# Attention and MLP-mixer on one core: the loads of the fourth batch's k and q moved ahead of a tail transpose on the DMA queue

The kernel runs on one core of one Trainium2 chip (trn2). The metric is device time in microseconds (us) of one execution, lower is better. A DMA queue is here the list of copies and transposes that the Sync engine (SP) issues, in program order.

## The reference

Eight batches go through a linear attention with cosine weights and then a token and channel mixer. Cut to what matters:

```python
def _attn_ref(q, k, v):                     # 8 batches x 8 heads x 576 rows x 64, float32
    theta = np.pi / 2.0 * pos / S
    def phi(x, c, s):
        r = np.maximum(x, 0.0)
        return np.concatenate([r * c, r * s], axis=-1)
    q_p, k_p = phi(q, cos_w, sin_w), phi(k, cos_w, sin_w)
    kv = np.einsum('bhsf,bhsd->bhfd', k_p, v)
    z = np.sum(k_p, axis=2)
    num = np.einsum('bhsf,bhfd->bhsd', q_p, kv)
    den = np.einsum('bhsf,bhf->bhs', q_p, z)[..., None] + 1e-06
    return num / den

def _moe_ref(x, w_tok1, w_tok2, w_ch1, w_ch2):          # 256 token, 1536 channel units
    h = np.maximum(x.transpose(0, 2, 1) @ w_tok1, 0.0) @ w_tok2
    u = x + h.transpose(0, 2, 1)
    return u + np.maximum(u @ w_ch1, 0.0) @ w_ch2
```

## The kernel before

The channel mixer of one batch fills TensorE for a period of some 27 us. The work for the next two batches is hooked into that period's slots (a slot follows each group of matmuls). In the first period the channel mixer of batch 0 runs, in the second that of batch 1; the first nm of batch 2 comes in slot 6 of the second. Batches are counted from 0 in the code and from one in the text, so "the fourth batch" is `3`. JA is 5, the blocks of 128 rows that a batch's 576 rows fill.

Names in the lines of the profile: PE is TensorE, ACT ScalarE, DVE VectorE, POOL GpSimd, SPq the Sync engine's DMA queue. qp and kp are the weighted features of q and k, qpT is qp transposed, kv is the product of kp and v, and nm that of qpT and kv. u is what the channel mixer takes in and uT its transpose; c_ps are the mixer's first matmuls, o_ps its second.

```python
    def load(b, t):                           # k, q or v of a batch: two copies, 640 + 512 KB
        x = raw_of(t, b)                      # k and q: two buffers by b % 2; v: one
        ...
            dmas.append(nc.sync.dma_start(out=x[par::2, :, :n * D], in_=...))

        def q_turn(self, j, n):               # batches 2 to 7: transposed by the DMA queue
            if self.b in Q_DMA:
                nc.sync.dma_start_transpose(out=self.qpT[:, j * H:(j + n) * H, :], in_=...)
                return
        ...
        def num(self, j):                     # nm: needs qpT and kv
            for h in range(H):
                nc.tensor.matmul(nm[...], self.qpT[:, j * H + h, :], self.kv[:, h, :D + 1], ...)
        ...
        def mix2(self, g, turn=True):         # last part, g = 2: the batch's last 64 rows
                ...
                if self.c == 1:
                    utb = one.tile([P, Dm], BF16, name="utb")
                    nc.gpsimd.tensor_copy(utb, u_tail[:, i, :])
                    nc.sync.dma_start_transpose(out=uT_tail[:, i], in_=utb)   # tail transpose

    def first_hooks(n, n2):                   # n: batch 1, n2: batch 2
        ...
        at(12, load, 2, "v")
        ...
        for g in range(3):
            at(19 + g, n.mix2, g)             # g = 2 in slot 21: the tail transpose
        at(19, n2.q_feature, 0)
        at(20, n2.q_feature, 1)
        at(21, load, 3, "k")
        at(21, load, 3, "q")
        ...
    # at the end of the period: the stores of batch 0, four copies of 256 KB

    def second_hooks(n, m):                   # n: batch 2, m: batch 3
        ...
        at(0, n.q_turn, 0, 2)                 # three transposes of batch 2's q
        at(1, n.q_turn, 2, 2)
        at(2, n.q_turn, 4, 1)
        at(5, n.kv_mm)
        at(5, load, 3, "v")
        at(5, load, 4, "k")
        at(5, load, 4, "q")
        for j in range(JA):
            at(6 + j, n.num, j)
        ...
        at(13, load, 4, "v")                  # ahead of batch 2's u transposes (mix2)
```

## Time and profile before

| | before |
|---|---|
| median of three runs | 287.91 us (286.62 to 288.2) |
| the profiled run | 286.91 us, span 285.1 us, mean granted TensorE clock 0.981 |
| TensorE busy | 265.3 us, 93% of the span |
| wait of the third batch's first nm | 7.91 us |

How to read it: TensorE is the bound over the whole span, so the question is only where it stands still and why. The wait is in TensorE's own timeline (start, length, line, operation, names, shapes, count; in brackets the idle time before it and what ended it):

```profile
69.72 1.02 PE L392 MATMUL c_ps<-uT,wc_135 128*128 128x512 bf16 x4
78.65 0.62 PE L280 MATMUL nm<-kv,qpT 128*128 128x65 bf16 x8 [7.91 <-DMA qpT<-qp]
```

The prediction below shows the page's rows, the chain of waits and the DMA queue around this wait.

### The profile page before, as it was taken

What the parts mean: (1) busy time and instruction counts of PE and PEld (TensorE: products, weight loads), DVE (VectorE), ACT (ScalarE), POOL (GpSimd) and SP (SyncE); (2) the same over time, 40 slices, a digit from 0 to 9 for tenths busy, and PEclk for the clock granted to TensorE, in tenths of its full rate; (3) what the DMA queues carried; (4) which work ended last, traced back from release to release, by engine and by line L of the source; (5) the groups of instructions that cost most, each with busy time, mean ns of one, the idle gap of its engine ahead of it and who ended that gap; (6) DMA issues with size and microseconds to landing.
All of it is one profiled execution on the core that took longest, in us unless ns stands there. A gap on an engine that the chain in (4) does not pass through costs nothing.

```text
span 285.1 us, 4653 instructions
## 1 busy us (share of the span) xinstructions
PE 265.3 (93%) x1834; PEld 133.0 (47%) x1834; DVE 168.0 (59%) x333; ACT 119.6 (42%) x176; POOL 55.3 (19%) x81
## 2 busy tenths in 40 slices
PE   8879989989099999999999999999999999999994
PEld 3454455444044454446444644464455444444443
DVE  4774884496055966794578459955866562322422
ACT  2973594339114733914490548055705201301300
POOL 4472420070003510250042004400200030000000
PEclk9999999999669999999999999999999999999999
DMA  6999998709999999999969994960493063003012
GB/s 212 318 165 288 356 210 260 255 20 286 284 232 359 238 227 277 344 207 212 347 185 217 254 365 94 196 165 2 90 218 101 0 94 126 21 0 149 0 51 97
DMA packets 78726, 53.62 MB, mean 188 GB/s; under 512 B 47792, under 2 KB 76016, under 8 KB 78704
## 3 DMA queue, kind: packets, MB, share of 16 engines
q1 hardware_dynamic: 74688, 49.06, 62.8%
q0 software_dynamic: 3616, 3.74, 8.2%
q10 hardware_dynamic: 400, 0.52, 0.5%
q8 instruction: 14, 0.23, 0.3%
q14 instruction: 8, 0.07, 0.1%
HBM read 35.78 MB, written 9.44 MB: 159 GB/s over the span
## 4 chain that ended last, share of the span: by engine, by line
PE 82%; DMA 7%; ACT 5%; DVE 3%; issue 1%; POOL 0%; ACTq 0%; POOLq 0%; DVEq 0%
PE c_ps L392 30%; PE o_ps L424 28%; PE u_ps L343 5%; PE nm L280 4%; DMA qpT<-qp 3%; DMA vt_77<-in_v_dram 3%; PE o_ps L404 3%; PE kv_ps L265 3%; ACT qp L236 2%; ACT qpT L256 1%; DVE x L288 1%; PE ut_ps L355 1%; PE o_ps L416 1%; PE b_1001 L300 1%; PE b_692 L300 1%; PE b_2301 L300 1%
## 5 line engine op out<-in xcount | busy, mean ns | idle before, releaser
L392 PE MATMUL c_ps<-uT,wc_135 128*128 128x512 bf16 x384 | 95.1, 384 | 1.1 <-ACT uT L376 1.1
L392 PEld LDWEIGHTS <-wc_135 128*128 128x128 bf16 x432 | 40.0, 98 | 44.4 <-issue 3.1
L348 POOL CAST ub<-u 128x1024 bf16<-128x1024 f32 x14 | 14.7, 1049 | 131.2 <-DVE u L345 91.7
L427 DVE TENSOR_TENSOR u<-o_ps,u 128x512 f32<-128x512 f32 x28 | 19.2, 687 | 21.5 <-PE o_ps L424 21.5
L288 DVE TENSOR_TENSOR x<-nm,den 128x512 bf16<-128x512 f32 x40 | 27.7, 691 | 1.4
L280 PE MATMUL nm<-kv,qpT 128*128 128x65 bf16 x320 | 17.2, 197 | 9.9 <-DMA qpT<-qp 7.9
L284 DVE TENSOR_SCALAR den<-nm 128x8 f32<-128x8 f32 x40 | 6.6, 165 | 31.7 <-PE nm L280 31.7
L280 PEld LDWEIGHTS <-qpT 128*128 128x128 bf16 x320 | 15.1, 100 | 21.0 <-DMA qpT<-qp 9.1
L345 DVE TENSOR_TENSOR u<-u_ps,x 128x1024 f32<-128x1024 f32 x16 | 19.5, 1221 | 5.1 <-PE u_ps L343 5.0
L223 POOL CAST vbf_125<-vt_77 128x512 bf16<-128x512 f32 x18 | 12.3, 725 | 24.0 <-DMA vt_77<-in_v_dram 22.3
L236 ACT ACTIVATE qp<-qt_79,bias_108,cos_t 128x512 bf16<-128x512 f32 x20 | 15.9, 804 | 0.0
L236 ACT ACTIVATE qp<-qt_76,bias_108,cos_t 128x512 bf16<-128x512 f32 x19 | 15.0, 802 | 0.3 <-DMA qt_76<-in_q_dram 0.3
L265 PEld LDWEIGHTS <-kp 128*128 128x128 bf16 x320 | 11.3, 97 | 3.5 <-issue 1.2
L404 PE MATMUL o_ps<-wc_139,h_441 128*128 128x512 bf16 x48 | 12.3, 379 | 0.0
L396 ACT ACTIVATE h_2730<-c_ps 128x512 bf16<-128x512 f32 x6 | 3.6, 597 | 20.6 <-PE c_ps L392 20.6
L236 ACT ACTIVATE qp<-qt_76,bias_108,sin_t 128x512 bf16<-128x512 f32 x15 | 12.0, 802 | 0.0
L236 ACT ACTIVATE qp<-qt_79,bias_108,sin_t 128x512 bf16<-128x512 f32 x15 | 12.0, 802 | 0.0
L215 DVE TENSOR_SCALAR kp<-kt_75,cos_t 128x512 bf16<-128x512 f32 x18 | 10.3, 570 | 2.7 <-DMA kt_75<-in_k_dram 2.7
L396 ACT ACTIVATE h_844<-c_ps 128x512 bf16<-128x512 f32 x9 | 5.1, 593 | 16.0 <-PE c_ps L392 16.0
L215 DVE TENSOR_SCALAR kp<-kt_78,sin_t 128x512 bf16<-128x512 f32 x20 | 11.6, 580 | 0.0
L138 PE MATMUL wm<-zero 128*128 128x512 bf16 x38 | 10.1, 429 | 1.3 <-POOL zero L70 1.3
L215 DVE TENSOR_SCALAR kp<-kt_78,cos_t 128x512 bf16<-128x512 f32 x20 | 11.3, 567 | 0.0
(151 smaller groups left out, 397.0 us busy)
## 6 DMA issues: line engine op xcount, KB each, us to landing
out_dram<-u SPq DMA_DIRECT2D x32, 256.0 KB, 2.6
vt_77<-in_v_dram SPq DMA_DIRECT2D x8, 640.0 KB, 9.4
vt_77<-in_v_dram SPq DMA_DIRECT2D x8, 512.0 KB, 8.6
kt_75<-in_k_dram SPq DMA_DIRECT2D x4, 640.0 KB, 5.6
qt_76<-in_q_dram SPq DMA_DIRECT2D x4, 640.0 KB, 8.1
kt_78<-in_k_dram SPq DMA_DIRECT2D x4, 640.0 KB, 6.4
qt_79<-in_q_dram SPq DMA_DIRECT2D x4, 640.0 KB, 8.5
kt_75<-in_k_dram SPq DMA_DIRECT2D x4, 512.0 KB, 4.6
```

Of the source, the lines that this page charges most:

```text
L215: eng.tensor_scalar(dst, src, scalar1=tab, scalar2=0.0, op0=ALU.mult, op1=ALU.max)
L236: nc.scalar.activation(self.qp[:, j, :, f, :], src, AF.Relu, bias=bias0, scale=tab[:, self.c, j:j + 1])
L265: nc.tensor.matmul(kv_ps[:, g, hh * (D + 1):(hh + 1) * (D + 1)], self.kp[:, j, h].rearrange("p f d -> p (f d)"), self.vb[:, j, h, :D + 1], ...
L280: nc.tensor.matmul(nm[:, h // HH, c0:c0 + D + 1], lw, self.kv[:, h, :D + 1], start=True, stop=True)
L288: nc.vector.tensor_mul(self.x[:, j, :].rearrange("p (g h d) -> p g h d", g=2, h=HH), nmv[:, :, :, :D], den_b)
L343: nc.tensor.matmul(u_ps[:, jj], w2[:, self.c, ki, 2 * g + jj, :], self.B1[:, ki, :], start=(ki == 0), stop=(ki == NT - 1))
L345: nc.vector.tensor_add(self.u[:, js, :], u_ps, self.x[:, js, :])
L348: nc.gpsimd.tensor_copy(self.ub[:, js, :], self.u[:, js, :])
L392: nc.tensor.matmul(c_ps, wc1[:, ki, mi * P:(mi + 1) * P], uT[:, :, ki, :], start=(ki == 0), stop=(ki == NCC - 1))
L404: nc.tensor.matmul(o_ps[j], h1[:, ki, j * P:(j + 1) * P], wc2[:, ki, :], start=(ki == 0), stop=(ki == NCH - 1))
L424: nc.tensor.matmul(o_ps, h1[:, ki, j * P:(j + 1) * P], wc2[:, ki, :], start=(ki == 0), stop=(ki == NCH - 1))
L427: nc.vector.tensor_add(u[:, j, :], o_ps, u[:, j, :])
```

## The change

The intent: k and q of the fourth batch fill buffers that have long been free, yet on the queue they stand behind the tail transpose, which waits for its input. Then they stand in front of the third batch's q transposes, which TensorE needs at once. Issued eight slots sooner, they go ahead of the tail transpose. The whole diff:

```diff
         at(19, n2.q_feature, 0)
         at(20, n2.q_feature, 1)
-        at(21, load, 3, "k")
-        at(21, load, 3, "q")
+        at(13, load, 3, "k")
+        at(13, load, 3, "q")
         if 1 in U_PE:
```

## The prediction

> **What bounds the kernel now.** I read the page first, for the engine that is busy and for slices in which it is not. The first row is TensorE's busy share in 40 slices of 7.1 us, the second its granted clock, the third the DMA engines:
> ```profile
> PE   8879989989099999999999999999999999999994
> ...
> PEclk9999999999669999999999999999999999999999
> DMA  6999998709999999999969994960493063003012
> ```
> TensorE is busy 265.3 of 285.1 us, so it is the bound. Three things stand out: TensorE's eleventh slice (71 to 78 us) is a 0, the only one; its clock fell in the eleventh and twelfth; and the DMA engines have a slice of 0 just before, the ninth (57 to 64 us). Nothing else in the row of the clock is low.
>
> Next I read the chain of work that ended last, in order of time, around those slices (start us, length us, what):
> ```profile
> 68.22 0.48 ACT h_844 L396
> 68.70 0.25 ACT qp L236
> 68.95 9.65 DMA qpT<-qp
> 78.60 0.05 issue
> 78.65 0.62 PE nm L280 x8
> 79.27 1.71 PE c_ps L392 x4
> 80.98 0.44 PE nm L280 x8
> 81.42 1.71 PE c_ps L392 x4
> 83.12 0.46 PE b_1001 L300 x2
> ```
> From 88 us to the end at 281 the chain is all TensorE with pieces of "issue" under 0.3 us. Before 88 us its largest piece by far is this transpose of the third batch's q on the DMA queue. It ends a TensorE wait of 7.91 us (the timeline's figure, 70.74 to 78.65), and the two groups of four c_ps matmuls after it take 1.71 us each where the same group takes 0.86 in the rest of the chain: half clock.
>
> Why is the transpose late? The DMA queue's own timeline (start, length of the issue, not of the transfer):
> ```profile
> 45.86 1.32 SPq L87 DMA_DIRECT2D vt_77<-in_v_dram  x2
> 61.87 1.27 SPq L365 DMA_TRANSPOSE uT_tail<-utb  x1
> 63.19 1.28 SPq L87 DMA_DIRECT2D kt_78<-in_k_dram  x2
> 64.52 1.48 SPq L87 DMA_DIRECT2D qt_79<-in_q_dram  x2
> 66.09 2.76 SPq L439 DMA_DIRECT2D out_dram<-u  x4
> 68.95 11.51 SPq L242 DMA_TRANSPOSE qpT<-qp  x3
> 80.56 1.43 SPq L87 DMA_DIRECT2D vt_77<-in_v_dram  x2
> ```
> The queue sat 14.7 us behind the tail transpose, which waits for its input (the queue's waits call it 15.7 us, L365 on POOL). When that came, k and q of the fourth batch, the stores of the first batch and the three q transposes all went out in one burst. Of the 11.51 us of the three transposes, the first alone took 7.56. The amounts of data tell the rest:
> ```profile
> 47.00:55.00 8.00, 8.00 (x57) 3.65 (x56) 4.10 (x12) 0.65 (x2) 0.00 (x0) 1.00 1.06 355
> 55.00:62.00 7.00, 6.67 (x43) 3.43 (x42) 5.50 (x7) 3.77 (x5) 2.85 (x4) 1.00 0.01 5
> ```
> (The last three columns are clock, DMA share, GB/s.) Loads ran at 355 GB/s to 55 us, then the DMA engines did nothing for 7 us while TensorE worked on, then they were full while TensorE stood still.
>
> **What the Trainium skill says.** "Perfetto Trace Analysis", section "DMA Instruction — HWDGE (DVE, Sync)": the reported span of a DMA issue starts when its semaphore waits are satisfied and ends when its descriptors are generated, and the data movement is not in it; a full descriptor buffer makes the transfer start before generation is over. I read the 7.56 us so: no semaphore wait, but descriptors that found no room behind 2.36 MB of loads and 1.05 MB of stores. The trace agrees: the same transpose issue of two column groups takes about 2.1 us (median of 18: 2.145) when the queue is free. "DMA: Bandwidth & Descriptors", "Queues, rings and completion order": on each DMA engine one queue's descriptors are consumed in ring order; so the order of issue matters, and the transpose landing 9.6 us after issue where the median is 4.5 agrees. "TensorE: Matmul & The Clock Gate", "Part 1: The HAM clock gate": after an idle window of about 3.4 us the clock is halved. Here it was granted 0.50 from 74 to 80 us, inside and after the only wait of that size; a wait of 1.10 us (before c_ps at 63.27) left it at 1.00.
>
> **The change part by part.** Nothing is removed or added: four DMA issues (two for k, two for q) move from slot 21 of the first period to slot 13.
> 1. *When they go.* The queue is free at 45.86+1.32 = 47.18, after v of the third batch (slot 12). The buffers they fill were last read by the second batch's features, which ended at 41.4 (ACT's last qp at 40.59+0.81). The copies of this queue share eight completion semaphores in turn, so each also waits for the landing of the one eight issues before it; in the new order those have all landed by then, here and for the stores and transposes after. So they issue at 47.2 to 49.9, without a wait.
> 2. *When they land.* k and q are each 640+512 KB, 2.36 MB together. In ring order behind the third batch they start at 55 us; 2.36 MB / 355 GB/s = 6.6 us, so they end near 61.6, in the hole that is there, or a microsecond or two later for the slowest engine. They are needed only at slot 13 of the next period, after 90 us now. The transfer is hidden both before and after; it is what it stands in front of that matters.
> 3. *What that does to the queue.* The tail transpose still goes at 61.87 (POOL's cast). Then the stores go 2.9 us sooner, from 63.2 (u is ready at 63.59, DVE 61.11+2.48) to 65.9. The first q transpose issues at 65.9, its input having been ready since 57.75. It has only 1.05 MB of stores ahead, landing near 68.4 (about 3 us after the last issue; median of all stores 2.6). Issue end about 68.5 to 69, landing 2.0 us later as now (78.60 against an issue end of 76.51): 70.5 to 71. Second: its input ends at 68.2 (ACT), landing near 73. Third: near 74.7.
> 4. *What TensorE waits for instead.* nm also needs kv:
> ```profile
> 71.44 0.61 ACT L270 CAST kv<-kv_ps 128x520 bf16<-128x520 f32 x1
> ```
> ACT is busy without a break before it (6.41 of the 7.47 us from 63.27), and nothing in its work changes. So nm can start at 72.1, not at 70.74: **the wait shrinks from 7.9 to about 1.4 us**, and 6.5 us go. The second transpose is needed by the third nm: 72.1 + two nm of 0.43 + two c_ps of 0.86 + b 0.46 = 75.1, two microseconds after it lands.
> 5. *Clock.* A 1.4 us wait is like the 1.10 us one, so the clock stays up. Two c_ps groups at 0.86 instead of 1.71 give 1.7, the first nm at 0.43 instead of 0.62 gives 0.2: 1.9 us.
> 6. *Given back.* The next loads now go at 80.56, 1.9 us after nm starts; in my sum they go near 72.7, 0.6 after it, but nm to the third nm is shortened by 1.9, so relative to TensorE's later work the DMA stream is some 0.6 us later (80.56-72.7 = 7.9 against 8.4). The u transposes behind it land about 0.9 us before the next period's c_ps needs them (98.7 and 100.6 by the trace's semaphore records, against 101.47), so that costs 0 to 0.5 us: 0.2.
>
> Sum: 6.5 + 1.9 - 0.2 = 8.2 us. 287.9 - 8.2 = **279.7 us**, 2.8% less. From 88 us on TensorE is the bound without a hole, so what is gained there stays gained.
>
> **The rivals.** *The transfer is hidden anyway, and nothing changes.* For it: k and q of the fourth batch are used 25 us later. Against: they are in ring order ahead of a transpose that ends a 7.9 us TensorE wait. It would leave 287. *The stores are the true obstruction.* 1.05 MB is 3 of the 9.4 us of traffic before the transpose; if the transpose must wait for every store's receipt, plus 2 us, it lands at 72 to 74 and the gain is 6 to 8. A similar place speaks for this in part: at 100.11 a q transpose behind 0.5 MB of stores landed after 4.9 us. That would make 280 to 282. *A new wait takes its place.* kv from ACT is counted; if the moved loads overrun 62 us, the tail transpose and the stores slip by as much, which there are 1 to 1.5 us of room for; 279.7 to 281. *DMA becomes the bound later.* It is near full from 66 to 150 us; but its total is the same, and 6.6 us of it move into a hole, so it has more room, not less; the u transposes' margin of 0.9 us is the weak place, worth 1 us.
>
> **Range and chances.** Best case, clock and wait as summed and nothing given back, and the spread of the runs (286.6 to 288.2): 278. Worst of the likely ones, transpose at 74.5 and the u transposes late: 283. Two per cent is 5.8 us, which needs the first nm before about 74.8; I give that 0.91. Slower has no mechanism that I can see: 0.01.
>
> **What would show it.** On the queue, k and q of the fourth batch at 47 to 50, before the tail transpose; DMA share near 1 from 55 to 61; the first q transpose near 66 with an issue of 3 us instead of 7.6; nm near 72 with a wait of about 1.4 us, put down to ACT kv rather than DMA; no low digits in the clock's row there; from there all TensorE pieces as now, 8.2 us sooner. The prediction is wrong if the loads don't go before 61.87, if the transpose still waits several microseconds behind the stores, or if the c_ps at the end of the second period begins to wait for uT.

## The result, and the profile after

The changed kernel takes 278.97 us (median of four runs, 278.3 to 279.09) against 287.63 us (four runs) before. The ratio is 0.970 (95% interval 0.967 to 0.973). Ratios here are the mean time of one kernel's fast runs over that of the other's of the same rounds, so they are not quite the ratio of the medians quoted. All of these runs were in the fast state.

The page's rows, as those of before in the prediction (40 slices, now of 6.9 us):

```profile
PE   8879998998799999999999999999999999999994
...
PEclk9999999999999999999999999999999999999999
DMA  6999997997999999999989968920890073003012
```

TensorE's slice of 0 is gone, and so is the DMA engines' slice of 0 before it, the ninth; the clock is full throughout. The DMA queue's timeline after:

```profile
48.02 4.62 SPq L87 DMA_DIRECT2D kt<-in_k_dram  x2
52.68 3.16 SPq L87 DMA_DIRECT2D qt<-in_q_dram  x2
62.13 1.28 SPq L365 DMA_TRANSPOSE uT_tail<-utb  x1
63.50 2.48 SPq L439 DMA_DIRECT2D out_dram<-u  x4
66.09 7.35 SPq L242 DMA_TRANSPOSE qpT<-qp  x3
73.53 1.44 SPq L87 DMA_DIRECT2D vt<-in_v_dram  x2
```

The loads went at 48 to 56 us instead of 63 to 66. The stretch from 55 to 62 us, which moved 5 GB/s before, now moves 356 (columns as in the prediction):

```profile
55.00:62.00 7.00, 6.62 (x40) 3.24 (x39) 5.26 (x7) 3.86 (x6) 2.59 (x3) 1.00 1.08 356
```

The three transposes now take 7.35 us to issue instead of 11.51 and start 2.9 us sooner. By the trace's semaphore records the first has an issue of 3.45 us and lands at 71.4; before it was 7.56 us and 78.6. The chain of work around the first nm, and TensorE's timeline there:

```profile
70.38 1.45 ACT h L396 x3
71.83 0.49 ACT kv L270
72.32 0.04 issue
72.36 0.43 PE nm L280 x8
```
```profile
72.36 0.42 PE L280 MATMUL nm<-kv,qpT 128*128 128x65 bf16 x8 [1.36 <-ACT kv L270]
72.62 1.02 PE L392 MATMUL c_ps<-uT,wc 128*128 128x512 bf16 x4
```

Where the chain went through the DMA for 9.65 us, it now goes through ACT. The two profiled executions can be laid side by side, at four events that both have (us from the start):

| event | before | after | shift | the stretch up to it changed by |
|---|---|---|---|---|
| first c_ps of the second period | 63.27 | 63.53 | +0.26 | +0.26 |
| first nm of the third batch | 78.65 | 72.36 | -6.29 | -6.55 |
| first kv_ps of the third period | 102.16 | 93.99 | -8.17 | -1.88 |
| last add | 281.09 | 273.16 | -7.93 | +0.24 |

So in these two executions 6.55 us come from the wait, 1.88 from the stretch after it, where matmuls had run at half clock, and 0.24 are given back later. Their whole times are 286.91 and 278.99, 7.9 us apart. The medians are 8.7 apart, since the profiled execution of before was one of its quicker ones; the runs of before spread over 1.6 us.

### The profile page after: what moved, and what is told of

It reads as the page before. It is cut to its first block, busy times and chain, and to the rows that moved or that the text cites. A ratio compares the mean times of both kernels' runs of the same rounds, so it can differ in the third digit from the quotient of the medians.

```text
span 277.2 us, 4630 instructions
## 1 busy us (share of the span) xinstructions
PE 262.3 (95%) x1813; PEld 132.1 (48%) x1834; DVE 168.7 (61%) x333; ACT 119.7 (43%) x176; POOL 55.6 (20%) x81
## 4 chain that ended last, share of the span: by engine, by line
PE 77%; ACT 9%; DMA 5%; DVE 5%; issue 2%; POOL 0%; ACTq 0%; POOLq 0%; DVEq 0%
PE c_ps L392 29%; PE o_ps L424 26%; PE b L300 5%; ACT qp L236 5%; PE u_ps L343 4%; PE nm L280 4%; DMA vt<-in_v_dram 3%; PE o_ps L404 3%; PE kv_ps L265 3%; DVE x L288 2%; DMA qpT<-qp 2%; ACT h L396 1%; ACT qpT L256 1%; PE ut_ps L355 1%; PE o_ps L416 1%
## 5 line engine op out<-in xcount | busy, mean ns | idle before, releaser
L392 PE MATMUL c_ps<-uT,wc 128*128 128x512 bf16 x384 | 93.4, 379 | 1.1 <-ACT uT L376 1.1
L396 ACT ACTIVATE h<-c_ps 128x512 bf16<-128x512 f32 x70 | 41.5, 596 | 112.7 <-PE c_ps L392 76.8
L424 PE MATMUL o_ps<-wc,h 128*128 128x512 bf16 x364 | 82.6, 379 | 0.5
L392 PEld LDWEIGHTS <-wc 128*128 128x128 bf16 x432 | 39.6, 97 | 43.9 <-issue 2.0
L424 PEld LDWEIGHTS <-h 128*128 128x128 bf16 x372 | 36.4, 98 | 43.9
L398 DVE TENSOR_SCALAR h<-c_ps 128x512 bf16<-128x512 f32 x38 | 26.1, 687 | 30.9 <-PE c_ps L392 30.9
L236 ACT ACTIVATE qp<-qt,bias,cos_t 128x512 bf16<-128x512 f32 x39 | 30.8, 803 | 0.6 <-DMA qt<-in_q_dram 0.6
L223 POOL CAST vbf<-vt 128x512 bf16<-128x512 f32 x33 | 22.2, 714 | 19.4 <-DMA vt<-in_v_dram 17.9
L236 ACT ACTIVATE qp<-qt,bias,sin_t 128x512 bf16<-128x512 f32 x30 | 24.1, 802 | 0.0
L215 DVE TENSOR_SCALAR kp<-kt,sin_t 128x512 bf16<-128x512 f32 x38 | 22.0, 580 | 0.0
```

What stands on the lines that cost most here:

```text
L215: eng.tensor_scalar(dst, src, scalar1=tab, scalar2=0.0, op0=ALU.mult, op1=ALU.max)
L223: eng.tensor_copy(self.vb[:, j, :, :D], src)
L236: nc.scalar.activation(self.qp[:, j, :, f, :], src, AF.Relu, bias=bias0, scale=tab[:, self.c, j:j + 1])
L392: nc.tensor.matmul(c_ps, wc1[:, ki, mi * P:(mi + 1) * P], uT[:, :, ki, :], start=(ki == 0), stop=(ki == NCC - 1))
L396: nc.scalar.activation(h1[:, mi, :], src, AF.Relu)
L398: nc.vector.tensor_relu(h1[:, mi, :], src)
```

## The experiments

Twelve kernels were run, the changed one once more among them, each beside the kernel before on the same chip. All gave correct outputs. The median of before was 287.3 to 287.4 us each time, and all verdicts use fast runs. The theory: the order on the queue decides, because a copy behind a waiting transpose inherits its wait and then stands ahead of what TensorE needs.

### The same order without the eight slots

```diff
+        at(21, load, 3, "k")
+        at(21, load, 3, "q")
         for g in range(3):
             at(19 + g, n.mix2, g)
-        at(21, load, 3, "k")
-        at(21, load, 3, "q")
```

> k and q of the fourth batch stay in slot 21 but are put ahead of the tail transpose within it. The DMA queue runs its instructions in order and waits for no TensorE slot, so the order on the queue becomes that of the change and the loads should go at 47 to 56 us all the same. Theory (the place in the queue's order is all of it): 279.0 us, the wait before nm about 1.4 us and put down to kv of ACT. Rival (it takes the eight slots): 287 us, the loads at 61 us or later.

Measured: 278.93 us, ratio 0.971 (0.969 to 0.974). The loads go out exactly as early as with the change, although their hook is again slot 21:

```profile
47.92 5.10 SPq L87 DMA_DIRECT2D kt<-in_k_dram  x2
53.06 3.16 SPq L87 DMA_DIRECT2D qt<-in_q_dram  x2
61.91 1.28 SPq L365 DMA_TRANSPOSE uT_tail<-utb  x1
```

So the slot number means nothing to this queue. It ran its list in order and waited for data and free buffers, not for the slots; what the change did is to swap two neighbours on the list.

### The tail transpose moved instead of the loads

```diff
+                    if self.b != 1:
+                        self.tail_turn()        # the transpose, now a method
...
         at(2, n.q_turn, 4, 1)
+        at(3, bt[1].tail_turn)
```

> The loads stay where they were in the kernel before; only the second batch's tail transpose is moved, behind the three q transposes. Theory (the tail transpose, which waits for its input until 62 us, kept the loads out of the empty stretch): the loads go at 47 to 56 us, 279.0 us, wait about 1.4 us. If the wait for kv of ACT is what is left, the 1.3 us that the tail transpose no longer takes ahead of the first q transpose bring nothing. Rival (the tail transpose is one more transfer in the burst and no more): 286 us.

Measured: 279.37 us, ratio 0.972 (0.970 to 0.974). The DMA queue and TensorE:

```profile
47.70 5.22 SPq L87 DMA_DIRECT2D kt<-in_k_dram  x2
52.97 3.16 SPq L87 DMA_DIRECT2D qt<-in_q_dram  x2
```
```profile
72.90 0.41 PE L280 MATMUL nm<-kv,qpT 128*128 128x65 bf16 x8 [1.35 <-ACT kv L270]
```

The loads went at 47.7, and nm waits 1.35 us for kv of ACT. With the obstacle taken away and the loads where they were, nearly the whole gain is there. This shows from the other side that the tail transpose kept the loads out of the empty stretch. That nothing stands ahead of the stores and the q transposes any more brings nothing, as expected where ACT's kv ends the wait.

### Only k moved

```diff
-        at(21, load, 3, "k")
+        at(13, load, 3, "k")
         at(21, load, 3, "q")
```

> Only k moves, q stays behind the tail transpose: 1.18 MB instead of 2.36 MB stand ahead of the q transposes. Theory (the bytes ahead set when the transpose can go): 1.18 MB at 355 GB/s is 3.3 us and two load issues are 1.4 us; the first q transpose lands near 74 to 75 instead of 78.6, the wait is 3.3 to 4.5 us, 281 to 284 us by whether the clock falls. Rival (any load there costs all): 287 us; rival (one of the two is free): 279 us.

Measured: 283.53 us, ratio 0.987 (0.983 to 0.991). TensorE's timeline:

```profile
75.39 0.43 PE L280 MATMUL nm<-kv,qpT 128*128 128x65 bf16 x8 [4.10 <-DMA qpT<-qp]
75.66 1.67 PE L392 MATMUL c_ps<-uT,wc 128*128 128x512 bf16 x4
77.13 0.65 PE L280 MATMUL nm<-kv,qpT 128*128 128x65 bf16 x8
77.59 1.87 PE L392 MATMUL c_ps<-uT,wc 128*128 128x512 bf16 x4
```

Half of the bytes gives about half of the gain: the wait is 4.10 us, between 7.91 and 1.36, inside the range of the expectation. Both rivals fall. The clock fell here too, and it fell at 75.89, half a microsecond after TensorE had gone back to work.

### Only the stores moved

```diff
-                for par in range(2):
-                    nc.sync.dma_start(out=out_rows(b, par, j - 1, 2), in_=u[...])
+                # batch 0: the two copies are kept in a list; release() issues them
...
         at(2, n.q_turn, 4, 1)
+        at(3, release)
```

> The loads stay where they were; the stores of the first batch are moved behind the q transposes. Theory: the 1.05 MB of stores are 3 of the 9.4 us and 2.8 us of issue; the first q transpose then lands near 74.5 to 75.5, wait 3.5 to 4.7 us, 282 to 284 us. Rival (the stores are the obstruction): 279 us. Rival (only the loads count): 287 us.

Measured: 285.58 us, ratio 0.994 (0.992 to 0.996), outside the 282 to 284 of the expectation. The DMA queue and TensorE:

```profile
66.07 12.02 SPq L242 DMA_TRANSPOSE qpT<-qp  x3
```
```profile
76.37 0.62 PE L280 MATMUL nm<-kv,qpT 128*128 128x65 bf16 x8 [5.54 <-DMA qpT<-qp]
```

The stores had been taken for 3 us or more of the wait. By the records, the first transpose's issue ends at 76.51 behind loads and stores, at 74.12 behind the loads alone (here), and at 69.54 behind the stores alone (the change). So taking the stores away is worth 2.4 us and taking the loads away 7.0. The loads are the obstruction, the stores a minor part; and 2.4 us less wait gave 1.7 us less time.

### The loads behind the q transposes

```diff
-        at(21, load, 3, "k")
-        at(21, load, 3, "q")
...
         at(2, n.q_turn, 4, 1)
+        at(2, load, 3, "k")
+        at(2, load, 3, "q")
```

> k and q of the fourth batch are put behind the three q transposes instead of ahead of the tail transpose. Theory (the change gains twice: nothing stands ahead of the transposes, and 6.6 us of transfer run in the empty stretch): nm starts near 72 as with the change, wait about 1.4 us, but v of the fourth batch and the fifth batch's loads come 6.6 us later, the u transposes of the third batch with them, and TensorE waits about 5 us for uT at the next period's start: 284 to 286 us. Rival (only what stands ahead of the q transposes counts, the empty stretch does not): 279 us.

Measured: 286.9 us, ratio 0.999 (0.997 to 1.001). TensorE's timeline at the first nm and at the next period's start:

```profile
72.06 0.41 PE L280 MATMUL nm<-kv,qpT 128*128 128x65 bf16 x8 [1.36 <-ACT kv L270]
...
99.25 1.89 PE L392 MATMUL c_ps<-uT,wc 128*128 128x512 bf16 x4 [6.29 <-DMA uT<-ub]
```

This is the run to learn from. The nm wait is as short as with the change, and the time is that of before. The 2.36 MB have only been moved 10 us on, where they stand ahead of the u transposes, and the wait came back a period later as 6.29 us. That is 1.3 us more than the 5 expected, and it took the clock with it again, for 6.83 us by the trace's clock records, which the expectation of 284 to 286 left out. So getting out of the transposes' way is half of the change. The other half is that the bytes cross in a stretch in which the DMA engines did nothing.

### The clock alone

30 matmuls on zeros fill the wait of the kernel before; their result is not used.

```diff
         for j in range(JA):
+        at(6, keep_warm, 30)                  # ahead of num(0) in slot 6
             at(6 + j, n.num, j)
```

> The kernel before, with 30 matmuls on zeros (216 ns each at full clock, 6.5 us) put into the wait ahead of the third batch's first nm; their result is not used. The wait itself stays: nm still starts near 78.6. Theory (1.9 us of the gain are the clock): the clock stays at 1.00, the two c_ps groups after nm take 0.86 instead of 1.71, and the time falls by 1.9 us to 285.5. Rival (the half clock lengthens only what has time to spare, and all of the gain is the wait): 287.4 us, no change.

Measured: 288.59 us, ratio 1.004 (1.002 to 1.006), slower than before. TensorE's timeline:

```profile
79.83 0.43 PE L280 MATMUL nm<-kv,qpT 128*128 128x65 bf16 x8 [1.70 <-DMA qpT<-qp]
80.10 1.02 PE L392 MATMUL c_ps<-uT,wc 128*128 128x512 bf16 x4
...
106.97 0.43 PE L280 MATMUL nm<-kv,qpT 128*128 128x65 bf16 x8 [1.97 <-DMA qpT<-qp]
```

The clock did stay at 1.00 here, and from nm to the third period's kv_ps it took 22.0 us instead of 23.5. But then nm of the fourth batch waits 1.97 us for its transposes, and at 107.69 the clock fell for 3.41 us. The theory fell as it was stated: in this order of the queue the warm clock brought no gain.

Why it was slower, and not merely the same, has two parts in the trace, and only the first is explained. The queue had hardly moved: counted from the second period's first c_ps, the fourth batch's first transpose was issued at 36.2 us instead of 36.8, so with the 4.9 us to its landing of before some 0.8 us could have been kept by my estimate. But it took 6.6 us to land. From 105.2 to 106.6 the DMA engines moved 10 GB/s, where from 105.0 to 106.5 before they moved 214. A 16 KB packet of the profile's instruction queue ran just ahead of this gap, at 104.90; before, it came at 108.71, after that landing. Whether the added matmuls brought it forward, and whether it made the gap, was not tested. The profiled execution is also the slowest of the 20 (290.15 us). By the clock listed for each run, nine of them lost it, at a median of 288.9; the eleven that did not still have 287.9, above the 287.3 of before.

Would the gain be kept if the queue had room? Two kernels asked that, with v of the fifth batch put behind the fourth batch's q transposes, without and with the 30 matmuls:

```diff
-        at(13, load, 4, "v")
...
         at(18, m.q_turn, 4, 1)
+        at(18, load, 4, "v")
```

> The kernel before, with v of the fifth batch (1.18 MB) issued behind the fourth batch's q transposes instead of ahead of the third batch's u transposes. This gives those transposes 3.3 us of room on the queue that TensorE, held at 78.65 and at half clock, can't use: 287.4 us, no change, unless v lands too late for its casts. It is the control of the next run.

> The same with the 30 matmuls on zeros in the wait. Theory (keeping the clock is worth 1.9 us, but in the run with the warm clock alone the DMA queue's stream took it back in a wait for qpT a period later): with room on the queue the 1.9 us are kept, 285.5 us, 0.66% below the control, and no wait over 0.5 us at the next period's start. Rival (the dummy matmuls cost as much as they bring): 287.4 us or more.

Measured: 289.78 us (ratio 1.009, 1.006 to 1.012) and 287.29 us (1.000, 0.998 to 1.003). The control failed as a control: it was to change nothing and cost 2.5 us, in part by a wait of 1.31 us for qpT at 137.6, a period further on. Another 0.6 us is the clock itself: its half rate lasted until 84.64, 5.6 us after nm, against 4.4 before. Against this control the warm clock is worth 2.5 us, and from nm to the third period's kv_ps it takes 21.6 us instead of 24.1; but that run too has a wait left, 1.32 us at 105.2, and with it the same gap: its transpose took 6.5 us to land, again behind a packet of the instruction queue (102.87). So the half clock's cost of about 2 us is seen in both profiles, and removing it pays against the control; against the kernel before it brought nothing in either order. How much of the change's own 1.88 us would have been lost without the move of the queue can't be told apart further: in the change both come together.

### What is left after the change

The changed kernel once more as control, and three steps on from it:

```diff
# kv on DVE (this edit is in all three)
-        at(5, n.kv_mm)
+        at(5, n.kv_mm, nc.vector.tensor_copy)
# first q transposes ahead of the stores (second and third)
-        at(0, n.q_turn, 0, 2)                 # second period
+        at(22, n2.q_turn, 0, 2)               # first period
-        at(15, m.q_turn, 0, 2)
+        at(14, m.q_turn, 0, 2)
# v of the fifth batch behind the fourth's q transposes (third)
-        at(13, load, 4, "v")
+        at(18, load, 4, "v")
```

> The changed kernel as it is, as the control of the next three on the same chip: 279.0 us, ratio 0.970.

> The changed kernel with kv of the third batch copied by DVE, which is idle then, instead of ACT. kv is ready near 71.0 instead of 72.3; nm then waits for the first q transpose (landed at 71.4) and starts 0.9 us sooner. Theory (the DMA queue's stream is now the limit up to the next period's start, where uT and qpT landed with nothing to spare): the 0.9 us come back as a wait there, 279.0 us. Rival (kv was what remained on the path): 278.1 us.

> As the run before, and the first q transpose of the third and of the fourth batch is issued ahead of the stores of the batch before. The first lands near 68.5, so nm starts with no wait over 0.3 us; the fourth batch's lands about 1.5 us sooner. uT still lands behind v of the fifth batch. Theory: about 1 us is kept, 278.0 us. Rival (all of the 1.7 us): 277.3 us.

> As the run before, and v of the fifth batch behind the fourth batch's q transposes, so that neither uT nor qpT waits behind 1.18 MB. Theory (the queue's stream is the limit): the 1.36 us of wait and the 0.3 us of the next period go, 277.4 us. Rival (something else than the queue sets the next period's start, or v now lands too late): 278 us or more.

| run | median us | ratio to before (95%) |
|---|---|---|
| the change again | 279.13 (279.00 to 279.59) | 0.971 (0.969 to 0.974) |
| kv on DVE | 278.53 (278.45 to 278.58) | 0.969 (0.967 to 0.971) |
| and first transposes ahead of the stores | 279.52 (279.45 to 279.90) | 0.973 (0.970 to 0.975) |
| and v behind | 278.96 (277.50 to 279.81) | 0.970 (0.966 to 0.973) |

TensorE's timelines of the first step and of the second:

```profile
71.66 0.43 PE L280 MATMUL nm<-kv,qpT 128*128 128x65 bf16 x8 [0.81 <-DMA qpT<-qp]
```
```profile
70.88 0.42 PE L280 MATMUL nm<-kv,qpT 128*128 128x65 bf16 x8
...
92.76 1.04 PE L392 MATMUL c_ps<-uT,wc 128*128 128x512 bf16 x4 [0.77 <-DMA uT<-ub]
```

With kv on DVE the wait is put down to the transpose, 0.81 us: kv and the transpose had come less than a microsecond apart. 0.6 us of the time went, and the runs of the two kernels don't overlap in this round (in its first round the changed kernel had runs of 278.30 to 279.09). My theory for this run, that the queue would take it all back, fell; the rival's 0.9 us was a little too much. In the second step nm starts with no wait, and the queue does take it back: 0.77 us for uT, and further on 0.31 and 0.66 for qpT. Neither expectation held, the time rose. In the third the waits at the period's start are gone, and one of 1.52 us for qpT turns up a period later, at 127.4; its theory of 277.4 fell too. But its six runs spread from 277.50 to 279.81 and the profiled one, 279.12, is among the slower, so what it is worth stays unclear. Only the first step is shown to be worth keeping; by the median it is the fastest version found, 0.2% under the change.

## Why the prediction was right

The measured 278.97 us lies 0.7 us from the 279.7 predicted. By its own steps:

1. **When the loads go.** Right in order and effect, wrong in length: predicted 47.2 to 49.9, measured 48.0 to 55.9. The issues themselves took 7.8 us instead of 2.7. Each found five copies still in flight; that this is the reason was not tested. Nothing stood behind them until 62, so it cost nothing.
2. **When they land.** Predicted near 61.6 or a little later for the slowest engine; the last landed at 64.0 by the records. The stretch of 55 to 62 us was filled at 356 GB/s, as predicted from 355.
3. **What it does to the queue.** The stores went at 63.50 (predicted 63.2), the first transpose at 66.09 (65.9), its issue took 3.45 us (about 3), it landed at 71.4 (70.5 to 71). One reading behind this was off: 2.145 us is the median of all 18 transpose issues, six of which have one column group (1.26 to 1.57). The twelve of two groups run from 1.70 to 7.56, median 2.77.
4. **What TensorE waits for instead.** kv of ACT, 1.36 us (1.4). The run with kv on DVE shows how close a second rival was: the transpose would have ended the wait 0.55 us earlier, no more.
5. **Clock.** The arithmetic was right, 1.88 us measured in the stretch after nm against 1.9. The reasoning behind it was not shown: it was added as a gain of its own, and in the warm run the clock alone brought none. That it came out right is partly luck: the same change moved the queue by 7.0 us (v of the fourth batch goes at 73.53 instead of 80.56). The half clock was also read too short, "from 74 to 80"; by the clock records it lasted from 72.81 to 83.05.
6. **Given back.** 0.24 us measured, 0.2 predicted. The weak place was expected at uT, with a margin of 0.9 us; by TensorE's timeline it was 0.7, since c_ps began at 101.30 and not at the 101.47 of the chain. The change used it up: uT landed at 93.07, 0.04 us before c_ps. So c_ps just did not wait there, and what was lost came mostly at the fourth batch's nm, whose qpT landed as it was needed.

Of the rivals, the stores as the true obstruction is refuted by the run that moved them alone, and the hidden transfer by the change itself. (The 9.4 us of traffic named there are 9.6 at the prediction's own 355 GB/s.) DMA as a later bound was taken too lightly. Four of the runs above (the loads behind, the warm clock, the first transposes ahead of the stores, and v behind) shortened a wait or kept the clock, and met a wait later.

## What to carry to other kernels

On an in-order queue the slot in the source is not a time: a copy behind an instruction that waits for compute inherits the wait. Put copies whose buffers are free ahead of such an instruction. Before counting what a shorter wait is worth, look at what the same queue brings next and whether the bytes have an empty stretch to go to; moved on by 10 us they can cost the same wait again. A TensorE wait long enough to lower the clock costs more than its own length (1.9 us more here), but don't count that surplus before seeing that the next transfers come sooner as well: where they did not, it was not gained.

## What the Trainium skill lacked or had wrong

- "TensorE: Matmul & The Clock Gate", "Part 1: The HAM clock gate", says that the clock halves after an idle window of about 3.4 us. The clock records here agree on the length: half clock lasted 10.24 us before (and with v behind alone), 6.83 in two of the runs and 3.41 in two others, whole multiples of 3.41. But a window need not be wholly idle: before the change the clock fell at 72.81, only 2.1 us after TensorE had stopped at 70.74, so 1.3 of the 3.41 us before it had been busy. In the run with only k moved it fell 0.5 us after TensorE had resumed, and in the run with the clock alone a wait of 1.97 us was enough. Cut from 60 to 270 us into stretches of 3.41 us that end where the clock records do, the traces show, among stretches at full clock, a fall after each with 1.97 us of idle or more and none after one with 1.80 or less. The 1.36 us of the change were below that.
- "Perfetto Trace Analysis", "DMA Instruction — HWDGE (DVE, Sync)", says that a full descriptor buffer makes the transfer start early; it does not say what a later issue pays. Here a transpose of 16 column blocks issues in 1.7 to 2.1 us at its quickest, in 3.45 behind 1.05 MB of stores, 7.56 behind 2.36 MB of loads and the stores, and 8.05 behind the loads alone, for which it started 2.9 us sooner. A plain load's issue, some 0.65 us with little in flight, took up to 3.03 in the changed kernel and 3.52 in the same order by slot 21.
- No page says that keeping the clock up by dummy matmuls can make a kernel slower. Here it did, by 0.4%. The profile shows the next transposes landing late (6.6 us after issue instead of 4.9); why they did is not shown.
